# One pool of six PSUM banks for scores, first feed-forward products, masks and transposes, with score visits of one to three slots

## The chip, the core and the metric

The kernel runs on one core of a Trainium2 chip. The metric is the device time in microseconds from the start to the end of one execution; the figure for a kernel is the median of several runs. The profile is one profiled execution, with times in us from its first instruction. PE is the tensor engine, PEld its weight loads, DVE the vector engine, ACT the scalar engine, POOL is GpSimd, and SP issues most of the transfers. Each engine works through its own instructions in the order in which they were written into the program.

## The reference

Attention with a block mask, then a feed-forward layer with a squared relu:

```python
# q, k, v: 4 batches x 8 heads x 768 positions x 64
scores = scale * q @ k.T
scores = where(mask, scores, -1e9)        # blocks of 32: neighbours, edges, 3 sampled blocks per row
attn   = softmax(scores)
x      = (attn @ v), heads side by side   # 3072 tokens x 512
out    = relu(x @ w_in) ** 2 @ w_out      # 512 -> 2048 -> 512
```

## The kernel before

**Attention.** The 32 pairs of batch and head are handled two heads at a time, so there are 16 units `u`, four to a batch. A *slot* is one unit, one range of queries and two or three chunks of 128 keys. In batch 0 the first 256 queries come in two ranges of 128 with three chunks of keys (16 slots of 2 x 384 scores); everywhere else a slot is 256 queries by two chunks of keys (132 slots of 2 x 512 scores). A slot's scores are keys by queries and fill two PSUM banks, one per head. `scores` (L381) writes them: each matmul contracts over 64 rows, and the two heads sit in the upper and lower half of the array. `exps` (L399) is one exponential on ACT for both banks, into an SBUF tile `pT`. `masks` (L405) multiplies `pT` with the mask on DVE; the first 16 slots instead add the mask inside the scores with extra matmuls (L395). `values` (L420) multiplies `pT` with the values and a column of ones, 65 columns per matmul, into a bank `po` that is held for one range of queries. `normalize` (L435) divides by the sum on DVE, and the result is transposed to `xT`: in batch 0 by PE (`x_transp`, L444), later by a transposing transfer.

**Feed-forward.** Tokens come in tiles `T`: for batch 0 two of 128 and two of 256, for each later batch two of 384. `hidden` (L478) multiplies one chunk of 128 of the 2048 columns of `w_in` with `xT`, four matmuls deep, into a bank `ph`. At tiles of 128 tokens two chunks share a bank (`per_unit`, L475). `relu` (L488), on ACT or DVE, moves the bank to an SBUF tile `r` in float32; `square` (L497), on POOL or ACT, makes the bfloat16 tile `g`. `output` (L521) sums `g` times `w_out` over the 16 chunks into a bank `py`, in eight parts; `out_copy` and `store` take it out.

**PSUM.** There are eight banks. Before, four belong to the pool `ps` (two score tiles of two banks each, also used for `mask_rows`, L302), two to `ph` (first products, and the transposes `pt` and mask tiles `pk` of the opening), one to `po` and one to `py`.

**What sets the order.** Nothing is ordered by hand. Every step is a `Task` with an engine or a choice of engines with estimated durations, a key (its priority), the tasks it depends on, and the buffers it takes (`get`) and gives back (`put`). `run_schedule` (L119) simulates the engines and picks again and again the task that could start first, ties broken by key; tasks with a key under 100 (attention) go ahead of the rest within a margin `AHEAD`. A small hash (`tie`, `SEEDS`) shifts the keys. When a task is picked, its function is called and its instructions are written into the program. So the constants, the number of buffers and the seeds determine each engine's order, and the chip then runs that order with its real durations.

`attend` (L606) makes the tasks of a *visit*: the scores of one or two slots written together, since PE changes between contraction over 64 and over 128 rows around a visit. Before, batch 0 has visits of one slot for its first 128 queries and of two for the rest, and the later batches visits of two. `PACE0` and `PACE` give the earliest time at which a visit of batches 1 to 3 may start. `prepare` (L560) makes loads, casts and transposes of a unit; in batches 1 to 3 the transposes are transfers.

The feed-forward tasks are made at the end (L688 to L726): for each tile the first products of this tile and the output parts of the tile before are interleaved by key, and all may run beside attention as soon as their `xT` is there.

Of the kernel before, what the change touches and what calls it, by code (L numbers as in the profile page):

```python
# [19 lines left out]
P = 128  # L20
# [5 lines left out]
def kernel(  # L26
# [27 lines left out]
    TWM = 384  # L54
# [5 lines left out]
    PT_BUFS, R_BUFS, G_BUFS, XT_BUFS = 6, 4, 2 * NF + 2, 3  # L60
# [3 lines left out]
    ps_s = ctx.enter_context(tc.psum_pool(name="ps_s", bufs=2))  # L64
    ps_o = ctx.enter_context(tc.psum_pool(name="ps_o", bufs=1))
    ps_h = ctx.enter_context(tc.psum_pool(name="ps_h", bufs=2))
# [9 lines left out]
    CB, GATES = 0.4, (6, 7)  # L76
    QT0, ADDED, ALONE = [(0, 128), (128, 128), (256, 256), (512, 256)], (0, 128), (0, 128)
# [5 lines left out]
    AHEAD = {"PE": 0.021, "DVE": 0.089, "ACT": 0.144, "POOL": 0.0, "SP": 0.0}  # L83
    LEAD = 9.733
    PACE0, PACE, SINGLE, MASK_AT = 43.352, 1.684, 1, 17.0

    class Buf:
        def __init__(self, pool):
            self.pool, self.holds, self.free = pool, 0, 0.0
# [4 lines left out]
    TIES = 2.757, 2.707  # L94
    SEEDS = (
            997007, 734824, 532673, 925841, 745989, 714641, 109461, 798098, 925326,
            634149, 527289, 224329, 653624, 743444, 608088, 229557, 928387, 381331,
            84432, 104783, 194889, 255966, 621276, 580226, 46894, 921115)
# [6 lines left out]
    class Task:  # L105
        def __init__(self, engs, key, fn, deps=(), get=(), put=(), after=0.0, mode=None, dma=0.0, late=None, bias={}, port=False):
            self.engs = engs if isinstance(engs, dict) else dict([engs])
            self.key, self.fn = key, fn
            self.deps, self.get, self.put = list(deps), list(get), list(put)
            self.after, self.mode, self.dma, self.late, self.bias = after, mode, dma, late, bias  # L110
            self.port = port
            self.end = self.eng = None
            self.order = len(tasks)
            self.key += TIES[0 if key < 300 else 1] * tie(self.order)
            for b in self.put:
                b.holds += 1
            tasks.append(self)

    def run_schedule(free, bufs, dma_free, mode=128):  # L119
        taken = {name: [] for name in bufs}  # L120
        port = {"DVE": (0.0, 0.0), "POOL": (0.0, 0.0)}
# [7 lines left out]

        while waiting or ready:  # L130
            now = [t for t in waiting if all(d.end is not None for d in t.deps)]
# [5 lines left out]
            for t in ready:  # L137
                r0 = t.after
                ok = True
                cnt = {}  # L140
                for b in t.get:
                    held = taken[b.pool]
                    at = len(held) + cnt.get(b.pool, 0) - bufs[b.pool]
                    cnt[b.pool] = cnt.get(b.pool, 0) + 1
                    if at >= 0:
                        if held[at].holds:
                            ok = False
                            break
                        r0 = max(r0, held[at].free)
# [3 lines left out]
                for e, us in t.engs.items():  # L153
                    r = max([r0, free[e]] + [seen(d, e) for d in t.deps])
# [6 lines left out]
                found.append((round(opt[1], 4), t.key, t.order, t, opt))  # L161
                if t.key < 100:
# [3 lines left out]
                       key=lambda c: c[:3], default=None)  # L166
            assert best is not None, "no task can start"
# [19 lines left out]
            for b in t.get:  # L187
                taken[b.pool].append(b)
# [65 lines left out]
    junk = ps_h.tile([P, 512], F32, name="junk", tag="h")  # L254
    for _ in range(N_WARM):
        nc.tensor.matmul(junk[:, 0:256], warm[:, 0:P], warm, start=True, stop=True)
# [45 lines left out]
    def mask_rows(c0, c1, e):  # L302
        mtile["R"] = ps_s.tile([P, 1024], F32, name="pb", tag="ps")[:, 0:c1 - c0]
# [7 lines left out]
    def mask_tile(n, c0, c1, e):  # L311
        pk = ps_h.tile([P, 512], F32, name="pk", tag="h")[:, 0:c1 - c0]
# [26 lines left out]
    def transp(u, w, ns, e):  # L339
        src = cast.pop((u, w, ns.start))  # L340
        pt = ps_h.tile([P, NCH, P], BF, name="pt", tag="h")
# [39 lines left out]
    def scores(slots, add, e):  # L381
        for a in slots:
            u, q0, w, cs = a
            i = u % NPB
            ps = ps_s.tile([P, 2, 512], F32, name="ps", tag="ps")
# [88 lines left out]

    def per_unit(T):  # L475
        return 2 if T[2] == P else 1

    def hidden(T, f, half, e):  # L478
        b, c0, w = T
        n = per_unit(T)  # L480
        if half == 0:
            htile[T, f] = ps_h.tile([P, TWM], F32, name="ph", tag="h")[:, 0:w * n]
        work_ = [(f + i, i, kc) for i in range(n) for kc in range(KM)]
        for f_, i, kc in work_[half * len(work_) // 2:(half + 1) * len(work_) // 2]:
            nc.tensor.matmul(htile[T, f][:, i * w:(i + 1) * w], w_in_sb[:, kc, f_ * P:(f_ + 1) * P], xT[b][:, kc, c0:c0 + w],  # L485
                             start=(kc == 0), stop=(kc == KM - 1))

    def relu(T, f, e):  # L488
        r = work.tile([P, TWM], F32, name="r", tag="r", bufs=R_BUFS)[:, 0:T[2] * per_unit(T)]
        src = htile.pop((T, f))  # L490
        if e == "ACT":
            A.activation(out=r, in_=src, func=AF.Relu)  # L492
        else:
            V.tensor_scalar(out=r, in0=src, scalar1=0.0, scalar2=None, op0=AOP.max)  # L494
        rltile[T, f] = r

    def square(T, f, e):  # L497
        g = work.tile([P, TWM], BF, name="g", tag="g", bufs=G_BUFS)[:, 0:T[2] * per_unit(T)]
        r = rltile.pop((T, f))
# [4 lines left out]
        for i in range(per_unit(T)):  # L504
            gtile[T, f + i] = g[:, i * T[2]:(i + 1) * T[2]]
# [12 lines left out]
    def y_pool(T, i):  # L518
        return "h" if T == TILES[-1] and i % 2 else "y"

    def output(T, i, ts, cs, part, e):  # L521
        if part == 0:
            pool, tag = (ps_h, "h") if y_pool(T, i) == "h" else (ps_y, "y")
            ytile[T, i] = pool.tile([P, d_model], F32, name="py", tag=tag)[:, 0:cs[1] - cs[0]]
# [14 lines left out]
    def T_(engs, key, f, *args, **kw):  # L539
# [5 lines left out]
              (3, 0, 0): 9.8, (3, 1, 0): 10.9, (1, 2, 0): 11.9, (2, 2, 0): 13.0, (3, 2, 0): 14.0}  # L545
    arrive.update({(u, 0, 2): (15.1, 15.8, 16.4, 17.1)[u] for u in range(HP)})
# [13 lines left out]
    def prepare(u):  # L560
# [17 lines left out]
        else:  # L578
            at = dict(after=arrive[u, 2, 0])
            late_q = first_of_tile[u, 2 * P]  # L580
            for w, ns in [(1, ns) for ns in (KEYS if u == 0 else (ALL,))] + [(0, ns) for ns in QRS]:
# [4 lines left out]
                qc, hb = Buf("qc"), Buf("h")  # L586
# [6 lines left out]
                t = T_(("PE", 0.06 * n), key + 1, transp, u, w, ns, deps=[c], get=[hb], put=[qc], mode=128)  # L593
# [12 lines left out]
    def attend(group, add):  # L606
        s = min(order.index(a) for a in group)
        bufs = {a: Buf("ps") for a in group}
# [3 lines left out]
        sc = T_(("PE", (0.44 if add else 0.22) * area), s, scores, group, add,  # L612
                deps=deps + (mr[:1 + (group[-1][1] + group[-1][2] > QW)] if add else []) + sc_all[-1:], get=[bufs[a] for a in group], mode=64,
                after=PACE0 + PACE * (s - N0) * (1.06 - 0.0006 * (s - N0)) if s >= N0 else 0.0)
        sc_all.append(sc)
        for a in group:
# [5 lines left out]
            ex = T_(("ACT", 0.2 + 0.82 * part), s, exps, a, deps=[sc], get=[pt], put=[bufs[a]])  # L622
# [4 lines left out]
            va = T_(("PE", 0.245 * part), s + 3.009, values, a, deps=[ex] + cv[u] + va_all[-1:] + (kws if po_pool(u, q0) == "y" else []),  # L627
# [23 lines left out]
    for i, (c0, c1) in enumerate(((0, QW), (QW, S))):  # L651
        rb_ = Buf("ps")
        t = T_(("PE", 0.11 + 0.11 * i), 5.0 if i else -90.0, mask_rows, c0, c1, after=9.8 if i else 4.6, get=[rb_], put=[], mode=32)
# [6 lines left out]
    for us in [range(b * HP, (b + 1) * HP) for b in range(B)]:  # L660
# [3 lines left out]
        if us[0] < HP:  # L664
            for c0, c1, at in MASKED:
                for n in range(NCH):
                    mb, w = Buf("h"), (c1 - c0) / 512
                    t = T_(("PE", 0.216 * w), (2 * n + 30 if c0 == 0 else 2 * n + 2), mask_tile, n, c0, c1, get=[mb], mode=128, after=at, deps=mr)
# [3 lines left out]
            while mine:  # L672
                q0 = mine[0][1]
                n = 1 if q0 in ALONE or len(mine) == 1 else 2
                attend(mine[:n], q0 in ADDED)
                mine = mine[n:]
        else:
            for i in range(0, len(mine) - 1, 2):
                attend(mine[i:i + 2], False)
            if len(mine) % 2:  # L680
                attend(mine[-1:], False)

    HID = {256: 0.22, 384: 0.325}
    RELU = {256: {"DVE": 0.424, "ACT": 0.39}, 384: {"DVE": 0.557, "ACT": 0.49}}
    SQ = {256: {"POOL": 0.613, "ACT": 0.42}, 384: {"POOL": 0.826, "ACT": 0.52}}
    sq_of, n_key = {}, 1000.0
    gbuf, hbuf = {}, {}
    for k_, T in enumerate(TILES + [None]):  # L688
# [4 lines left out]
        for _, kind, x in sorted(both, key=lambda z: z[:2]):  # L693
# [3 lines left out]
            if kind == 0:  # L697
# [3 lines left out]
                hb, rb, gb = Buf("h"), Buf("r"), Buf("g")  # L701
                gbuf[x] = gb
                last_use = c0 + t[2] == S and f == NF - 1
                h0 = T_(("PE", HID[w]), n_key - 0.5, hidden, t, f, 0, deps=need + [wl[f * NWP // NF], wl[(f + per_unit(t) - 1) * NWP // NF]],
                        get=[hb], mode=128)
                h1 = T_(("PE", HID[w]), n_key - 0.6, hidden, t, f, 1, deps=[h0],
                        put=[xb[b]] if last_use else [], mode=128)
                rr = T_(RELU[w], 200, relu, t, f, deps=[h1], get=[rb], put=[hb], bias={"ACT": 0.276})
                sq = T_(SQ[w], n_key, square, t, f, deps=[rr], get=[gb], put=[rb], bias={"ACT": 0.533})
                sq_of.update({(t, f + i): sq for i in range(per_unit(t))})  # L710
            else:
# [7 lines left out]
                yy = T_(("PE", 0.432 * n), n_key, output, t, i, ts, cs, part,  # L719
# [3 lines left out]
                if part == NY - 1:  # L723
# [5 lines left out]
                 {"ps": 2, "po": 1, "h": 2, "y": 1, "pT": PT_BUFS, "r": R_BUFS, "g": G_BUFS, "ys": YS_BUFS,  # L729
# [31 lines left out]
```

## Time and profile before

Three runs took 273.89, 274.52 and 274.79 us; the median is 274.52. The profiled execution has a span of 273.3 us.

| group | count | busy us | mean ns |
|---|---|---|---|
| exponentials, 1024 wide, ACT (L402) | 132 | 127.8 | 1022 |
| exponentials, 768 wide over two banks, ACT (L402) | 16 | 12.4 | 812 |
| mask products, DVE (L409) | 132 | 102.3 | 789 |
| output products, 512 wide, PE (L526) | 368 | 97.2 | 379 |
| first products, 384 wide, PE (L485) | 384 | 78.7 | 326 |
| value products, PE (L431) | 1152 | 53.9 | 193 |
| scores, 256 wide, PE (L391) | 528 | 40.5 | 272 |
| relus 384 / 256 wide, ACT (L492) | 46 / 35 | 21.8 / 12.5 | 497 / 404 |
| relus 384 / 256 wide, DVE (L494) | 50 / 13 | 27.6 / 5.5 | 556 / 421 |
| squares 384 / 256 wide, POOL (L503) | 62 / 33 | 59.4 / 27.6 | 963 / 848 |
| squares 384 / 256 wide, ACT (L501) | 34 / 15 | 17.9 / 6.3 | 525 / 430 |

Busy time of a group is the union of its instructions, so it is less than the count times the mean where instructions overlap. Matmuls are pipelined and their recorded ends are modelled: the distance between the starts of two neighbours tells more than the length of one. An engine that is idle costs nothing unless the one that sets the pace waits for it.

### The profile page before, as it was taken

The page shows a single profiled execution, that of the slowest core. Times are in us where ns is not written, and L with a number is a line of the kernel's source. Part 1 is how long each engine was busy: PE and PEld are TensorE (multiplying, and loading weights), DVE is VectorE, ACT ScalarE, POOL GpSimd, SP SyncE. Part 2 cuts the span into 40 slices and gives each one's busy share as a digit, 9 for nine tenths or more (in the row PEclk, how much of TensorE's full clock was granted, in tenths as well). Part 3 has the DMA queues.
Part 4 walks back from the last instruction along what each step waited for, and adds up shares of the span by engine and source line. Part 5 has one row for each costly group of instructions (what it writes and reads, how often), then busy time and mean ns, then how long its engine had stood idle before and what let it go on. Part 6 is the DMA issues. An engine that isn't in the chain of part 4 may idle for free.

```text
span 273.3 us, 7473 instructions
## 1 busy us (share of the span) xinstructions
PE 265.3 (97%) x3032; PEld 163.4 (60%) x3032; DVE 190.2 (70%) x380; ACT 207.6 (76%) x321; POOL 109.9 (40%) x138
## 2 busy tenths in 40 slices
PE   8889999999999999999999999999999999999995
PEld 5658766676666555565556555555555555555544
DVE  7778779989786768889666877786666775434400
ACT  3788999999999879999998799889999881010111
POOL 3194651457545227444420270441411414666410
PEclk9999999999999999999999999999999999999999
DMA  6999999999990285499711132355210111111112
GB/s 180 374 226 196 201 264 288 304 300 339 192 232 14 83 156 159 79 251 245 218 56 51 55 77 50 79 108 60 67 52 19 50 20 50 38 40 41 38 70 83
DMA packets 51882, 36.92 MB, mean 135 GB/s; under 512 B 30984, under 2 KB 48904, under 8 KB 51848
## 3 DMA queue, kind: packets, MB, share of 16 engines
q1 hardware_dynamic: 47080, 31.86, 43.9%
q0 software_dynamic: 4224, 4.19, 9.7%
q8 instruction: 23, 0.38, 0.6%
q10 hardware_dynamic: 544, 0.39, 0.5%
q14 instruction: 11, 0.09, 0.1%
HBM read 27.26 MB, written 6.29 MB: 123 GB/s over the span
## 4 chain that ended last, share of the span: by engine, by line
PE 83%; DMA 9%; POOL 2%; SPq 2%; ACT 2%; issue 1%; ACTq 0%
PE py L526 30%; PE ph L485 29%; PE po L431 12%; PE ps L391 12%; DMA w_out_sb<-in_moe_w_out_dram 6%; DMA vs<-in_v_dram 3%; SPq L226 2%; POOL w_in_sb L365 1%; ACT pT L402 1%; POOL w_out_sb L368 1%; POOL VT L200 0%; ACT ys L198 0%; ACT xT L198 0%; PE pk L313 0%; PE po L448 0%
## 5 line engine op out<-in xcount | busy, mean ns | idle before, releaser
L402 ACT ACTIVATE pT<-ps 128x1024 bf16<-128x1024 f32 (+1 forms) x148 | 140.2, 1000 | 11.2 <-PE ps L391 7.5
L503 POOL TENSOR_TENSOR g<-r 128x384 bf16<-128x384 f32 (+1 forms) x95 | 87.0, 923 | 120.4 <-DVE r L494 61.7
L409 DVE TENSOR_TENSOR pT<-pT,MK 128x1024 bf16<-128x1024 bf16 x132 | 102.3, 789 | 16.4 <-ACT pT L402 15.9
L485 PE MATMUL ph<-xT,w_in_sb 128*128 128x384 bf16 (+2 forms) x640 | 106.4, 294 | 0.0
L526 PE MATMUL py<-w_out_sb,g 128*128 128x512 bf16 (+1 forms) x400 | 100.7, 371 | 0.3 <-DMA w_out_sb<-in_moe_w_out_dram 0.2
L485 PEld LDWEIGHTS <-w_in_sb 128*128 128x128 bf16 x640 | 52.1, 97 | 28.7 <-issue 5.0
L431 PEld LDWEIGHTS <-pT 128*128 128x128 bf16 x1152 | 47.4, 98 | 18.6 <-issue 5.3
L431 PE MATMUL po<-VT,pT 128*128 128x65 bf16 x1152 | 53.9, 193 | 1.5 <-POOL VT L200 1.2
L494 DVE TENSOR_SCALAR r<-ph 128x384 f32<-128x384 f32 (+1 forms) x63 | 33.1, 528 | 31.4 <-PE ph L485 28.8
L526 PEld LDWEIGHTS <-g 128*128 128x128 bf16 x400 | 36.2, 98 | 28.3 <-issue 2.9
L391 PE MATMUL ps<-QK 64*128 64x256 bf16 (+1 forms) x624 | 47.3, 263 | 0.5 <-ACT pT L402 0.5
L198 ACT COPY ys<-py 128x512 f32<-128x512 f32 (+1 forms) x23 | 13.1, 570 | 38.0 <-PE py L526 37.8
L391 PEld LDWEIGHTS <-QK 64*128 64x128 bf16 x624 | 24.9, 94 | 23.0 <-issue 19.4
L492 ACT ACTIVATE r<-ph 128x384 f32<-128x384 f32 (+1 forms) x81 | 34.3, 457 | 3.0 <-PE ph L485 2.8
L501 ACT ACTIVATE g<-r 128x384 bf16<-128x384 f32 (+1 forms) x49 | 24.1, 496 | 6.0 <-DVE r L494 4.8
L200 POOL CAST VT<-vs 128x768 bf16<-128x768 f32 x15 | 13.8, 918 | 26.4 <-PE po L431 14.5
L441 DVE TENSOR_TENSOR xq<-po,rs 128x256 bf16<-128x256 f32 (+1 forms) x52 | 21.0, 404 | 1.8
L439 DVE RECIPROCAL rs<-po 128x4 f32<-128x4 f32 (+1 forms) x52 | 9.2, 177 | 13.5 <-PE po L431 13.2
L200 DVE CAST qc<-qs 128x768 bf16<-128x768 f32 (+2 forms) x18 | 12.6, 703 | 0.2 <-DMA qs<-in_q_dram 0.2
L200 DVE CAST qc<-ks 128x768 bf16<-128x768 f32 (+1 forms) x15 | 9.0, 603 | 1.9 <-DMA ks<-in_k_dram 1.8
L395 PE MATMUL ps<-R,oh 64*128 64x128 bf16 x96 | 6.7, 216 | 0.0
L343 PE MATMUL pt<-identb,qc 128*128 128x128 bf16 x48 | 5.0, 228 | 1.1 <-DVE QK L200 0.8
(51 smaller groups left out, 62.9 us busy)
## 6 DMA issues: line engine op xcount, KB each, us to landing
vs<-in_v_dram SPq DMA_DIRECT2D x16, 384.0 KB, 6.4
out_dram<-ys SPq DMA_DIRECT2D x23, 256.0 KB, 2.1
ks<-in_k_dram SPq DMA_DIRECT2D x15, 384.0 KB, 5.0
qs<-in_q_dram SPq DMA_DIRECT2D x12, 384.0 KB, 4.1
w_in_sb<-in_moe_w_in_dram POOLq DMA_DIRECT2D x4, 512.0 KB, 7.9
w_out_sb<-in_moe_w_out_dram POOLq DMA_DIRECT2D x4, 512.0 KB, 16.0
qs<-in_q_dram SPq DMA_DIRECT2D x4, 256.0 KB, 8.4
xT<-xq SPq DMA_TRANSPOSE x36, 2.3
```

Source lines behind the costliest of these rows:

```text
L200: (V if e == "DVE" else G).tensor_copy(out=out, in_=in_)
L391: nc.tensor.matmul(ps[:, h, j * w:(j + 1) * w], QK[i][hs, 1, ksl], QK[i][hs, 0, qsl], start=j == 0, stop=not add, skip_group_check=True)
L402: A.activation(out=pT[:, :, 0:n], in_=stile.pop(a)[:, :, 0:n], func=AF.Exp, scale=scale)
L409: V.tensor_tensor(out=pT, in0=pT, in1=m[:, None].broadcast_to([P, 2, len(cs), w]), op=AOP.mult)
L431: nc.tensor.matmul(po[:, qc, h, :], pT[:, h, j * w + qc * P:j * w + (qc + 1) * P], VT[i][:, h, n, 0:VW], start=(n == 0 and qc == 0 and h = ...
L441: V.tensor_tensor(out=xq, in0=po[:, :, :, 0:D], in1=rs.broadcast_to([P, n, 2, D]), op=AOP.mult)
L485: nc.tensor.matmul(htile[T, f][:, i * w:(i + 1) * w], w_in_sb[:, kc, f_ * P:(f_ + 1) * P], xT[b][:, kc, c0:c0 + w], start=(kc == 0), stop= ...
L492: A.activation(out=r, in_=src, func=AF.Relu)
L494: V.tensor_scalar(out=r, in0=src, scalar1=0.0, scalar2=None, op0=AOP.max)
L501: A.activation(out=g, in_=r, func=AF.Square)
L503: (G if e == "POOL" else V).tensor_mul(out=g, in0=r, in1=r)
L526: nc.tensor.matmul(ytile[T, i], gtile[T, f][:, ts * P:(ts + 1) * P], w_out_sb[:, f, cs[0]:cs[1]], start=(f == 0), stop=(f == NF - 1))
```

## The change

The pools `ps` and `ph` become one set of three pairs of banks, `X[0]` to `X[2]`, six banks in all. A task asks for `X1` (one bank) or `X2` (a pair), and the scheduler's `bank` gives it the place that comes free first. Four things follow from it:

- Scores (`X2`) can have three slots in PSUM at once instead of two. `GROUPS` sets the number of slots in a visit by batch and range of queries: one in batch 0, two in batch 1, three in batches 2 and 3.
- First products of tiles of 384 tokens take a pair and cover two chunks, so that one relu handles 768 columns over two banks; smaller tiles fill one bank with 512 columns (`per_unit` 4 and 2). The squares stay 384 or 512 wide. The first products of a pair are written in four parts and may be interleaved with other work (`yields`, `HOLD`).
- Transposes, masks and every second output of the last tile take an `X1`.
- The scheduler's constants are others (`AHEAD`, `LEAD`, `PACE0`, `PACE`, `TIES`, `SEEDS`, the preference of relus and squares for their engines, the key of `values`), so the order of all engines changes.

What it is for: buffers that go where they are needed, fewer and larger relus, and fewer changes of the array between 64 and 128 rows in the later batches.

```diff
-    TWM = 384
+    TWM = 768
-    PT_BUFS, R_BUFS, G_BUFS, XT_BUFS = 6, 4, 2 * NF + 2, 3
+    PT_BUFS, R_BUFS, G_BUFS, XT_BUFS = 6, 4, 34, 3
-    ps_s = ctx.enter_context(tc.psum_pool(name="ps_s", bufs=2))
+    ps_x = ctx.enter_context(tc.psum_pool(name="ps_x", bufs=1))
-    ps_h = ctx.enter_context(tc.psum_pool(name="ps_h", bufs=2))
...
+    GROUPS = (1, 1, 1), (2, 2, 2), (3, 3, 3), (3, 3, 3)
-    AHEAD = {"PE": 0.021, "DVE": 0.089, "ACT": 0.144, "POOL": 0.0, "SP": 0.0}
-    LEAD = 9.733
-    PACE0, PACE, SINGLE, MASK_AT = 43.352, 1.684, 1, 17.0
+    AHEAD = {"PE": 0.043, "DVE": 0.108, "ACT": 0.176, "POOL": 0.0, "SP": 0.0}
+    LEAD = 5.943
+    HOLD = 0
+    PACE0, PACE, SINGLE, MASK_AT = 39.28, 1.726, 1, 17.0
...
+        def bank(pool, now, gone):
+            n = 2 if pool == "X2" else 1
+            best = None
+            for c in range(0, 6, n):
+                mine = [cells[i] for i in range(c, c + n)]
+                if any(i in gone for i in range(c, c + n)) or any(b and b.holds for b in mine):
+                    continue
+                r = max([now] + [b.free for b in mine if b])
+                o = cells[c ^ 1]
+                k_ = (round(r, 4), n == 1 and not (o and o.holds), c)
+                if best is None or k_ < best[0]:
+                    best = (k_, c, r)
+            return best
...
+                if t.yields and not relaxed and due - HOLD < opt[1]:
+                    continue
...
+    X = [ps_x.tile([P, 1024], F32, name=f"X{i}") for i in range(3)]
+
+    def bank_of(b):
+        return X[b.at // 2][:, b.at % 2 * 512:(b.at % 2 + 1) * 512]
...
-            ps = ps_s.tile([P, 2, 512], F32, name="ps", tag="ps")
+            ps = X[bufs[a].at // 2].rearrange("p (h c) -> p h c", h=2)
...
-            va = T_(("PE", 0.245 * part), s + 3.009, values, a, ...
+            va = T_(("PE", 0.245 * part), s + 2.023, values, a, ...
...
-                n = 1 if q0 in ALONE or len(mine) == 1 else 2
-                attend(mine[:n], q0 in ADDED)
...
+            n = min(len(mine), GROUPS[us[0] // HP][mine[0][1] // QW])
+            if n == 3:
+                n = sum(a[:2] == mine[0][:2] for a in mine)
+            attend(mine[:n], us[0] < HP and mine[0][1] in ADDED)
...
     def per_unit(T):
-        return 2 if T[2] == P else 1
+        return {P: 4, QW: 2, S // 2: 2}[T[2]]
...
-                h0 = T_(("PE", HID[w]), n_key - 0.5, hidden, t, f, 0, deps=..., get=[hb], mode=128)
-                h1 = T_(("PE", HID[w]), n_key - 0.6, hidden, t, f, 1, deps=[h0], ...)
-                rr = T_(RELU[w], 200, relu, t, f, deps=[h1], get=[rb], put=[hb], bias={"ACT": 0.276})
-                sq = T_(SQ[w], n_key, square, t, f, deps=[rr], get=[gb], put=[rb], bias={"ACT": 0.533})
+                wide = w > 512
+                hb, rb = Buf("X2" if wide else "X1"), Buf("r")
+                parts = 4 if wide else 2
+                for part in range(parts):
+                    hd.append(T_(("PE", HID[w] / parts), n_key - (0.6 if part else 0.5), hidden, t, f, part, parts, hb, ...,
+                                 mode=128, yields=not part))
+                rr = T_(RELU[w], 200, relu, t, f, deps=[h1], get=[rb], put=[hb], bias={"ACT": 0.092})
+                for i in range(0, per_unit(t), n):
+                    sq = T_(SQ[n * t[2]], n_key, square, t, f, i, n, deps=[rr], get=[gb], put=[rb], bias={"ACT": 0.673})
```

## The prediction

> **What bounds the kernel now.** I read the page's busy table first, then busy time by stage, then the waits, then single instructions in order of time. The page's own lines:
>
> ```profile
> PE 265.3 (97%) x3032; PEld 163.4 (60%) x3032; DVE 190.2 (70%) x380; ACT 207.6 (76%) x321; POOL 109.9 (40%) x138
> PE   8889999999999999999999999999999999999995
> ACT  3788999999999879999998799889999881010111
> ```
>
> The tensor engine (PE) is busy nearly everywhere, ScalarE (ACT) nearly everywhere until the last fifth. To see which sets the pace, I cut the span at the first scores of 256 queries (24 us), of batches 1, 2 and 3 (59, 112, 168) and after the last scores (223). The columns are the window, its length, and each engine's busy time:
>
> ```profile
> 5.00:24.00 19.00, 16.53 (x347) 12.87 (x348) 14.69 (x46) 14.70 (x25) 9.46 (x13) 1.00 1.06 275
> 24.00:59.00 35.00, 33.98 (x511) 24.50 (x507) 29.56 (x61) 33.55 (x60) 15.15 (x18) 1.00 1.12 272
> 59.00:112.00 53.00, 53.00 (x651) 33.74 (x649) 41.50 (x76) 48.73 (x78) 25.96 (x30) 1.00 0.71 164
> 112.00:168.00 56.00, 56.00 (x632) 32.62 (x628) 43.39 (x81) 51.70 (x77) 21.10 (x20) 1.00 0.48 126
> 168.00:223.00 55.00, 55.00 (x614) 31.44 (x608) 39.30 (x74) 48.88 (x69) 14.85 (x14) 1.00 0.28 58
> 223.00:273.00 50.00, 47.01 (x284) 25.70 (x280) 17.91 (x33) 8.21 (x14) 21.27 (x26) 1.00 0.15 51
> ```
>
> From 59 us on PE is never idle (53.00 of 53.00 and so on). Before 59 us ACT is nearly full as well (33.55 of 35.00 in the second row), and this is where PE loses time. The waits of PE alone, longest first:
>
> ```profile
> PE po L431 <- POOL VT L200: 1.2, 1, 1.2
> PE pt L343 <- DVE QK L200: 0.8, 2, 0.5
> PE ps L391 <- ACT pT L402: 0.5, 2, 0.3
> ```
>
> These are only part: matmul ends are modelled, so I counted starts. In order of time around a visit to the scores (start, length, engine, line):
>
> ```profile
> 132.25 1.14 PE L485 MATMUL ph<-xT,w_in_sb 128*128 128x384 bf16 x6
> 133.32 0.61 PE L391 MATMUL ps<-QK 64*128 64x256 bf16 x8
> 133.86 0.60 PE L526 MATMUL py<-w_out_sb,g 128*128 128x512 bf16 x2
> ```
>
> One 384-wide matmul takes 0.326 us, so six in 1.14 start (1.14 - 0.326) / 5 = 0.163 apart. 132.25 + 6 x 0.163 = 133.23, but the scores start at 133.32: 0.09 lost. Eight scores in 0.61 with 0.27 for the last pair are 4 pairs 0.11 apart, 0.44 in all, yet the next matmul comes after 0.54: 0.10 lost. So one visit to the scores costs 0.19 us beyond its matmuls.
>
> By the same reading of starts, one matmul costs 0.216 us at 512 columns, 0.162 at 384, 0.109 at 256, 0.055 at 128, 0.055 for a 256-wide score (two run at a time), 0.029 for a 128-wide one, and 0.0295 for a value product. Summed over all 3,032 that is 243.1 us; 78 visits x 0.19 add 14.8: **257.9 us of PE work**. PE runs from 1.2 to 270.0, 268.8 us, so it loses 10.9. Up to batch 1's first scores at 59.07 the work is 49.3: there it loses 59.07 - 1.2 - 49.3 = 8.6, of which some 1.4 is the slow pace of the 14 warm-up matmuls. After that 208.5 us of work take 210.9; the losses there are crumbs.
>
> **What the Trainium skill says.** "TensorEngine Tiling (Array Packing)", Key Properties: changing the tiling mode drains the array. The trace agrees: 0.09 into and 0.10 out of the 64-row scores. "Perfetto Trace Analysis", Identifying the Most-Contended Engine: matmul busy share is no measure of headroom. Agreed: PE reads 97%, but 10.9 us of its span are not work. The same page, Optimizing Scalar/DVE Operations: each ACT or DVE instruction carries a fixed access cost, so larger ones gain. Agreed: a relu on ACT takes 404 ns at 256 columns and 497 at 384, so 0.73 ns per column and some 218 fixed.
>
> **The change part by part.**
>
> *Visits.* I counted both instruction orders that the scheduler writes. The matmuls are the same 3,032 in kind and number. Visits go from 78 to 74: batches 2 and 3 need 12 each instead of 18, but batch 0 splits its pairs into singles. 4 x 0.19 = 0.76 us saved, on the path.
>
> *PE work before batch 1.* In the new order 52.3 us of PE work stand ahead of batch 1's first scores (49.3 before): a stretch of 162 matmuls, 12.2 us without a visit, stands at the end of batch 0. With three score buffers before the first 256-wide scores, and singles after it, the array gets first feed-forward products in while ACT works on exponentials. Against this, ACT must be no slower there. Its counts from the first 256-wide exponential to batch 1: before 24 exponentials, 18 relus of 256, 8 squares of 256, 4 masks, 5 copies to xT, 2 output copies; after 24, 12 of 512, 5 of 512, 3, 4, 1. Two exponentials take 1.92 us together at 1.02 each, so an instruction counts its length less 0.1. The row means 1.022, 0.404, 0.430, 0.384, 0.36, 0.589 give before 39.7 - 61 x 0.1 = 33.6 us, which is what the window shows (33.55). After, with relus of 512 at 0.59 (404 + 256 x 0.73) and squares of 512 at 0.62 (0.430 and 0.525 at 256 and 384, extended): 37.9 - 49 x 0.1 = 33.0. So ACT would reach batch 1 some 0.6 us sooner, at 58.5, if the opening were the same. PE: 1.2 start + 1.4 slow pace + 52.3 = 54.9; waits for loads and first operands that no order removes (1.2 for VT in part, 0.8, the 24-row mask matmuls and their mode) I take as 3.6, from the seven pauses that I find before 24 us: 58.5 too. Two engines that both must be on time rarely are; I put batch 1's first scores at 58.8. PE's loss before it is then 58.8 - 1.2 - 52.3 = 5.3 instead of 8.6: **3.3 us saved**.
>
> *Wide relus.* Half as many relus, at 768 over two banks: no row shows one on ACT. Below: 497 + 384 x 0.73 = 0.78 us; above: two of 384, 0.99. The 768-wide exponential over two banks takes 0.812; I take 0.80. Relus now nearly all run on ACT (65 of 72; 81 of 144 before), DVE drops from 63 to 7 and gets 17 output copies instead of 2. With lengths less 0.1, ACT does 42 us in batch 1 against 46.2 of PE work, 53 against 61.0 in batch 2, 48 against 55.0 in batch 3 (all up to the last scores): 87 to 92%, where it was 89 to 92%. Nothing on the path. In the tail ACT gets 13 relus and 13 squares, about 15 us of 42: hidden under PE.
>
> *Visits of three.* The new wait: three slots need all three bank pairs, so nothing of the first product can be written until an exponential has freed a pair, and the next visit needs the relu done. The cycle: the first slot's scores are readable 0.48 us after the visit starts (0.22 issue, rest drain), three exponentials 0.90 apart, relu 0.80, release 0.06: 0.48 + 2.7 + 0.8 + 0.06 = 4.04. The shortest cycle of PE in the new order has 3.49 + 0.66 + 0.19 = 4.34. With two relus and a square between, 4.04 + 0.7 + 0.41 = 5.15 against 5.7. First product behind slot 0: free at 0.48 + 1.02 + 0.06 = 1.56; PE has scores to 0.75 and usually four output matmuls to 1.61. Value and output products queue behind that wait, and ACT's relu behind them. So the slack is 0.05 to 0.3 us per visit. Bounds: 0, and 0.2 for each of 24 visits, 4.8. I take 0.5 in all.
>
> Sum: 0.76 + 3.3 - 0.5 = 3.6 us: 274.5 - 3.6 = **270.9 us**.
>
> **Rivals.**
> 1. *The early gain is not had.* ACT, at 33.55 of 35, holds PE back by the same 59 - 49.3 = 9.8, so moved-up work only pushes batch 1 later, to 62. Only the visits remain: 274.5 - 0.8 = 273.7. For it: ACT's own saving is 0.6 alone. Against: PE's pauses lie beside ACT work, and the new order puts matmuls there.
> 2. *Triples stall.* If each of 24 visits waits 0.2 us and the 17 single visits of batch 0 wait as much more, with the early gain halved: 274.5 - 0.8 - 1.6 + 4.8 + 3.4 = **280**; with 24 x 0.2 alone and no early gain 278.5. For it: slack 0.05 at the first product. Against: ACT's share falls in batches 1 and 2.
> 3. *The opening shrinks too*, since scores no longer wait for the second buffer: all pauses but load waits go, batch 1 starts at 57.5: 269.4.
>
> **How the numbers follow.** Forecast 0.56 (with its spread up to 272.5), rival 3 0.15, rival 1 0.14, rival 2 or milder stalls 0.15. The range runs from 268.8 (rival 3, with no stalls) to 274.2, rival 1 with a little stall; only rival 2 and the extreme of rival 3 lie outside. Faster 0.78 (forecast, rival 3 and the lucky half of rival 1), same 0.09, slower 0.13.
>
> **What would show it.** Right: batch 1's scores start at 58 to 59.5 with more first-product matmuls before them; 74 visits; PE without pauses from there on, 207 us to its end; ACT fuller in the tail. A 768-wide relu near 0.80. Wrong: PE waiting on ACT at the first product (`ph`) after visits of three, batch 1 starting past 61, or relus well over 0.9 us.

## The result, and the profile after

The changed kernel takes 277.41 us (median; 276.76 to 277.65), the kernel before 274.34 beside it: a ratio of 1.0108 [1.0083, 1.0134], slower by 3.1 us. The forecast was 270.9, faster by 3.6.

Most runs of one kernel lie within 1 us of its median; the 19 of the kernel before beside run 5 spread from 273.0 to 276.3. The profile of before has a long span for its kernel (273.3; the median of 19 runs is 272.3), that of after a short one (274.6; the median of four is 275.4). So the two profiles differ by 1.3 us where the kernels differ by 3.1.

The busy table and the slices of the kernel after:

```profile
PE 261.5 (95%) x2992; PEld 165.8 (60%) x3032; DVE 166.0 (60%) x339; ACT 224.2 (82%) x294; POOL 87.2 (32%) x110
PE   7989999889998999999999999999999999999995
ACT  3789999868997999999899989899798988646511
```

DVE has lost 24 us of work and ACT has gained 17, as the change of the relus intends. New are the slices with an 8 in PE's row at 48 to 62 and at 82 us, and with them a 6 in ACT's row at 55 us: both engines idle at the same time. (PE's count is 2,992 because records are missing from this trace, not matmuls from the program.) Busy time by stage, cut at the same events as before (first scores of 256 queries, of batches 1, 2 and 3, last scores):

```profile
5.00:22.70 17.70, 16.00 (x333) 12.54 (x331) 13.60 (x42) 14.11 (x25) 8.70 (x12) 1.00 1.06 279
22.70:62.80 40.10, 37.29 (x547) 26.52 (x549) 30.01 (x65) 35.30 (x50) 15.26 (x14) 1.00 1.15 275
62.80:111.20 48.40, 46.89 (x594) 30.28 (x602) 38.08 (x70) 44.10 (x54) 18.93 (x19) 1.00 0.52 145
111.20:173.00 61.80, 60.58 (x654) 36.91 (x666) 39.79 (x73) 57.10 (x72) 18.93 (x22) 1.00 0.48 122
173.00:228.00 55.00, 54.04 (x593) 33.10 (x604) 35.47 (x68) 49.18 (x61) 12.35 (x15) 1.00 0.26 60
228.00:274.60 46.60, 43.00 (x267) 23.96 (x266) 5.21 (x9) 22.58 (x34) 10.98 (x14) 0.99 0.14 49
```

Batch 1's first scores start at 62.8, not at 58.8 as forecast and not at 59.1 as before. In the second row neither PE (37.29 of 40.10) nor ACT (35.30) is full. The waits of PE, longest first, show a kind that the kernel before did not have: first products (L541) that wait for a relu on ACT (L550). And the waits of ACT show the reverse, relus that wait for first products:

```profile
PE X L541 <- ACT r L550: 2.5, 4, 0.8
PE py L585 <- issue: 1.9, 12, 0.2
PE X L308 <- DVE bm L298: 1.2, 1, 1.2
```

```profile
ACT r L550 <- PE X L541: 19.9, 32, 2.1
ACT ys L246 <- PE py L585: 5.3, 2, 4.2
```

To see where PE's time went, I priced its matmuls as in the prediction (0.216 us for 512 columns and so on, 0.19 per visit, missing records filled in) and took each stage's work from its length. What is left is PE's loss.

| stage, up to | before: work, loss | after: work, loss |
|---|---|---|
| first scores of 256 queries | 17.41, 5.72 | 16.57, 4.97 |
| batch 1 | 32.30, 2.45 | 35.69, 4.39 |
| batch 2 | 52.01, 0.65 | 46.27, 2.18 |
| batch 3 | 55.37, 0.68 | 61.03, 0.66 |
| last scores | 54.56, 0.59 | 54.89, 0.44 |
| end of PE | 46.70, 0.38 | 42.70, 0.38 |
| all | 258.35, 10.47 | 257.15, 13.02 |

In the profile after, forty records are missing, so the table is good to some 0.25 us. Counted instead from the order of the matmuls in the two programs, its first two rows are 17.23, 5.90 and 32.08, 2.67 before, and 16.38, 5.15 and 35.91, 4.18 after; the work before batch 1 is then the 49.3 and 52.3 of the prediction, and all work differs by 0.76, the four visits. By either count what is lost in addition is lost between 22.7 and 111 us, 3.0 to 3.5 us more there than before. The losses of the stages with visits of three are those of before. A second profile of the same kernel (the run *after_again* below) gives 5.47, 4.34 and 2.18 in the first three rows, so this is no draw of one execution.

### The profile page after: what moved, and what is told of

It reads as the page before. It is cut to its first block, busy times and chain, and to the rows that moved or that the text cites. A ratio compares the mean times of both kernels' runs of the same rounds, so it can differ in the third digit from the quotient of the medians.

```text
span 274.6 us, 7322 instructions
## 1 busy us (share of the span) xinstructions
PE 261.5 (95%) x2992; PEld 165.8 (60%) x3032; DVE 166.0 (60%) x339; ACT 224.2 (82%) x294; POOL 87.2 (32%) x110
## 4 chain that ended last, share of the span: by engine, by line
PE 86%; DVE 4%; ACT 4%; issue 2%; DMA 2%; SPq 1%; ACTq 0%; DVEq 0%
PE X L541 30%; PE py L585 27%; PE po L483 12%; PE X L443 12%; PE X L585 2%; DMA ks<-in_k_dram 2%; ACT r L550 1%; ACT pT L454 1%; DVE pT L461 1%; DVE QK L248 1%; SPq L274 1%; PE X L365 1%; PE po L500 1%; PE X L395 1%; PE X L447 0%
## 5 line engine op out<-in xcount | busy, mean ns | idle before, releaser
L454 ACT ACTIVATE pT<-X 128x1024 bf16<-128x1024 f32 (+1 forms) x148 | 137.8, 1006 | 7.9 <-PE X L443 5.3
L461 DVE TENSOR_TENSOR pT<-pT,MK 128x1024 bf16<-128x1024 bf16 x132 | 93.6, 729 | 24.3 <-ACT pT L454 23.5
L562 POOL TENSOR_TENSOR g<-r 128x384 bf16<-128x384 f32 (+1 forms) x65 | 59.2, 913 | 149.2 <-ACT r L550 128.1
L541 PE MATMUL X<-xT,w_in_sb 128*128 128x384 bf16 (+2 forms) x640 | 99.9, 294 | 2.9 <-ACT r L550 2.5
L585 PE MATMUL py<-w_out_sb,g 128*128 128x512 bf16 (+1 forms) x328 | 87.6, 374 | 3.4 <-issue 1.9
L541 PEld LDWEIGHTS <-w_in_sb 128*128 128x128 bf16 x640 | 54.3, 97 | 33.1 <-issue 6.7
L550 ACT ACTIVATE r<-X 128x768 f32<-128x768 f32 (+1 forms) x65 | 48.6, 754 | 22.4 <-PE X L541 19.9
L443 PE MATMUL X<-QK 64*128 64x256 bf16 (+1 forms) x624 | 46.6, 264 | 0.8 <-DVE MK L373 0.2
L248 DVE COPY ys<-py 128x512 f32<-128x512 f32 x17 | 11.6, 685 | 27.6 <-PE py L585 27.6
L246 ACT COPY ys<-py 128x512 f32<-128x512 f32 (+1 forms) x6 | 3.3, 558 | 5.5 <-PE py L585 5.3
L447 PE MATMUL X<-R,oh 64*128 64x128 bf16 x96 | 6.7, 216 | 0.0
```

The costliest lines, as they stand in the source:

```text
L248: (V if e == "DVE" else G).tensor_copy(out=out, in_=in_)
L443: nc.tensor.matmul(ps[:, h, j * w:(j + 1) * w], QK[i][hs, 1, ksl], QK[i][hs, 0, qsl], start=j == 0, stop=not add, skip_group_check=True)
L454: A.activation(out=pT[:, :, 0:n], in_=stile.pop(a)[:, :, 0:n], func=AF.Exp, scale=scale)
L461: V.tensor_tensor(out=pT, in0=pT, in1=m[:, None].broadcast_to([P, 2, len(cs), w]), op=AOP.mult)
L541: nc.tensor.matmul(htile[T, f][:, i], w_in_sb[:, kc, (f + i) * P:(f + i + 1) * P], xT[b][:, kc, c0:c0 + w], start=(kc == 0), stop=(kc == K ...
L550: A.activation(out=to, in_=src, func=AF.Relu)
```

## The experiments

**1. The bank that has been free longest.** The first suspect: the scheduler's `bank` gives out the place that comes free first, perhaps one whose relu has only just ended. The whole order is planned first, then written, with the oldest free place for each buffer. All engines keep their order.

```diff
-            t.fn(e)
+            plan.append((t, e))
+        write(plan)
...
+                        age = max([freed[id(m)] for m in mine if m], default=0)
+                        spots.append((age, c))
+                    b.at = min(spots)[1]
```

> The changed kernel with the order of every engine kept instruction by instruction; only the place in PSUM of each buffer differs: the bank or pair that has been free longest, instead of the lowest one that the scheduler reckons free at that moment. Theory 1 (first products wait because they are put into a bank whose relu the scheduler reckons done and the chip has not done): PE's waits for relus on ACT fall from 2.5 us to under 0.5, batch 1's first scores come at 60.5 instead of 62.8, the whole takes 274.8 to 275.8. Rival (ACT's throughput of relus and squares holds the stretch, whichever bank is used): batch 1 stays at 62.5 or later and the time within 0.5 us of the changed kernel's 277.4.

Measured: 276.90 us (276.62 to 277.45), ratio 1.0102 [1.0076, 1.0127]: at most 0.5 us of the 3.1, and the two intervals overlap. PE's waits for relus on ACT fall from 2.5 to 1.8 us and not below 0.5, and batch 1 starts at 63.5. So the age of the bank does not account for the loss. (This run moved pairs of banks as well, and its program has more of the waits found below, 55 against 50, so it does not weigh the age alone.)

**2. The wide relu cut in two.** If one relu of 768 columns over two banks holds both too long, two of 384 free the first earlier.

```diff
-            A.activation(out=to, in_=src, func=AF.Relu)
+        for i in range(n) if n * w > 512 else (slice(None),):
+            if e == "ACT":
+                A.activation(out=to[:, i], in_=src[:, i], func=AF.Relu)
```

> The changed kernel with each relu of 768 columns over two banks written as two relus of 384, on the same engine and in the same place; all else in the same order. If ACT's wide relus do no harm and save their fixed part (theory): 47 more instructions of 0.40 less 0.31 of a wide one's saved half, some 0.12 us each, so ACT gets 5 to 6 us more work in batches 2 and 3; with ACT at nine tenths there, PE begins to wait and the time rises by 2 to 5 us to 279.5 to 282. Rival (the two-bank relu itself is slow or holds banks too long and is where the time went): the time falls below 276.5, since the first bank comes free earlier.

Measured: 278.44 us (277.15 to 280.49), ratio 1.0161 [1.0115, 1.0207]. From batch 1's first scores to the end of PE it takes 208.55 us, as the changed kernel does (208.56). The first wide relu runs at 103 us, so what this run loses more stands ahead of all that was edited, and the intervals overlap. Neither forecast came true. The wide relus do not cause the loss, and they gain nothing either: the forecast gave ACT 5 to 6 us more work without them, but ACT is busy 224.0 us in this profile, with 47 more instructions, and 224.2 in that of the kernel after (the relus of 768 columns by themselves take 38.2 us, their halves 41.0).

**3. Other seeds for the changed kernel.** Is the order merely an unlucky one? The seeds were searched anew, to an order whose planned end is within 0.5 us.

```diff
-            621053, 621053, 621053, 162164, 486097, 621053, 621053, 88936, 279485,
...
+    SEEDS = (959464, 225077, 897217, 946755, 474903, 41602, 596199, 225377, ...
```

> The changed kernel with other seeds in the tie-breaking hash, searched until the scheduler reckons about the same end (0.5 us later), so another order of the same kind. If the loss comes from the mechanism (buffers reused the moment the scheduler reckons them free, batch 0's attention ahead of batch 1's operands): again slower than its reckoning, 276 to 279. If it was the luck of one order (rival): anywhere from 271 to 280, and as likely below the kernel before as above.

Measured: 278.39 us (278.08 to 278.51), ratio 1.0151 [1.012, 1.0181]. Batch 1's scores start at 65.5 us: another order, the same kind of loss in the same place.

**4. Other seeds for the kernel before.** Its seeds in reverse.

```diff
-            997007, 734824, 532673, 925841, 745989, 714641, 109461, 798098, 925326,
...
+    SEEDS = (921115, 46894, 580226, 621276, 255966, 194889, 104783, 84432, ...
```

> The kernel before with its seeds in reverse order and nothing else: an order nobody selected. The scheduler reckons it 5.0 us later than with its own seeds. If orders count for as much as the change (order-luck rival): 277 to 281, more than the whole difference to explain. If orders hardly count on the chip: within 1.5 us of 274.3.

Measured: 276.45 us (275.89 to 278.28), ratio 1.0074 [1.0049, 1.01], between the two forecasts. An unsearched order costs the kernel before 2 us; orders matter, but run 3 shows that one other searched order does not mend the changed kernel.

**What the single instructions say.** The timeline of the kernel after, in the stretch without visits before batch 1 (start, length, engine, line; in brackets the wait). Lines of other work are left out:

```profile
51.33 0.59 ACT L550 ACTIVATE r<-X 128x512 f32<-128x512 f32 x1
51.43 0.88 PE L541 MATMUL X<-xT,w_in_sb 128*128 128x128 bf16 x9
...
51.95 0.63 ACT L560 ACTIVATE g<-r 128x512 bf16<-128x512 f32 x1
...
52.48 0.58 ACT L550 ACTIVATE r<-X 128x512 f32<-128x512 f32 x1
...
53.09 0.63 ACT L560 ACTIVATE g<-r 128x512 bf16<-128x512 f32 x1
53.11 0.60 PE L541 MATMUL X<-xT,w_in_sb 128*128 128x256 bf16 x4 [0.81 <-ACT r L550]
```

The last line is the second half of a first product in bank 3 (`X[1]`, upper half). It waits until 53.06 for a relu that reads *bank 2*, the lower half of the same `X[1]`. Its own first half, among the nine matmuls from 51.43, did not wait: it had been written into the program before that relu, the second half after it. The compiled program says the same: each wait names a semaphore and a value, and the instruction that raises it can be looked up. In the changed kernel 50 waits (21 of PE, 15 of ACT, 14 of DVE) name an instruction that touches only the *other* bank of the same tile. (A wait that stands on an instruction of its own is counted with the instruction behind it.) In the kernel before there are none: there every one-bank buffer is a tile of its own. So the theory: the program's dependencies are kept per tile `X[i]`, not per bank, and two unrelated buffers in its halves run one after the other. The scheduler's own plan, which knows no such waits, ends PE at 266.1; replayed with them, at the planner's durations, the order ends PE at 271.7; measured is 271.4. The changed kernel even looks for such neighbours: of banks that are free by the same time, `bank` gives a one-bank buffer the one beside a bank in use (the second term of `k_`), so that pairs stay whole.

**5. Other pairs.** The order stays the same on every engine; each buffer's place comes from a list, searched so that the two halves of one tile are seldom in use together.

```diff
+    PLACES = ("0245240420142042014520142350124204201420420452402024052024020...
...
-            t.fn(e)
+            plan.append((t, e))
+        at = iter(PLACES)
+        for t, e in plan:
+            for b in t.get:
+                if b.pool in ("X1", "X2"):
+                    b.at = int(next(at))
+            t.fn(e)
```

> The instructions of the changed kernel in its order on every engine; only the bank that each one-bank buffer gets is another: chosen so that the two banks of one 1024-wide tile X[i] are seldom in use at once. In the changed kernel 50 waits are on an instruction that touches only the OTHER bank of the same tile (21 of TensorE, 15 of ScalarE, 14 of VectorE); here 26 are left, and none stands in the stretch between the end of batch 0's attention and batch 1's first scores. False sharing (the theory after three runs): the two banks of one tile are tracked as one thing, so a first product waits for the relu of its neighbour bank and that relu for the product: replaying the order with the planner's own durations gives an end of TensorE at 271.7 with such waits (measured 271.4) and 267.2 with this choice; batch 1's scores at about 60 instead of 62.8, a time of 272 to 273.5. Rival (ScalarE and TensorE in step because one unit of 512 costs both about the same, or late operands of batch 1): the choice of bank means nothing, batch 1's scores at 62.5 to 63.5, 276.5 to 277.5.

Measured: 274.06 us (273.31 to 275.41, 14 runs), ratio 0.9989 [0.9968, 1.0009]. The choice of places alone is worth 3.3 us, about all that the change had lost; the forecast for it (272 to 273.5, batch 1's scores at about 60) was too good: they start at 61.3. The same place in the timeline (its lines stand 9 further down):

```profile
51.53 0.60 ACT L559 ACTIVATE r<-X 128x512 f32<-128x512 f32 x1
51.79 1.65 PE L550 MATMUL X<-xT,w_in_sb 128*128 128x128 bf16 x19
...
52.16 0.63 ACT L569 ACTIVATE g<-r 128x512 bf16<-128x512 f32 x1
...
52.70 0.58 ACT L559 ACTIVATE r<-X 128x512 f32<-128x512 f32 x1
...
53.31 0.63 ACT L569 ACTIVATE g<-r 128x512 bf16<-128x512 f32 x1
...
53.39 1.04 PE L550 MATMUL X<-xT,w_in_sb 128*128 128x256 bf16 x8
```

Nineteen matmuls in a row, across the same relus and squares, without a wait. The waits of PE, longest first, no longer hold a first product behind a relu on ACT:

```profile
PE py L594 <- issue: 1.9, 12, 0.2
PE X L317 <- DVE bm L307: 1.2, 1, 1.2
PE X L452 <- DVE MK L382: 0.5, 1, 0.5
PE po L492 <- POOL VT L257: 0.4, 1, 0.4
PE X L550 <- DVE r L561: 0.3, 1, 0.3
```

And the stretch from the last scores of batch 0 to the first of batch 1, which holds the same matmuls, first in the kernel after, then with other pairs (window, length, busy PE, PEld, DVE, ACT, POOL):

```profile
47.70:62.80 15.10, 13.26 (x166) 10.39 (x166) 7.62 (x15) 11.08 (x19) 5.63 (x6) 1.00 1.16 301
```

```profile
48.38:61.28 12.90, 12.80 (x166) 10.40 (x166) 7.32 (x15) 10.68 (x19) 5.84 (x6) 1.00 1.16 303
```

PE is now full there: 12.80 of 12.90, so the stretch is 2.2 us shorter. Ahead of it, from the first scores of 256 queries, other pairs takes 25.62 us and the kernel after 24.98, and there ACT is as full as PE or fuller (kernel after first, then other pairs):

```profile
22.72:47.70 24.98, 24.01 (x381) 16.13 (x385) 22.39 (x51) 24.20 (x32) 9.63 (x9) 1.00 1.15 259
```

```profile
22.76:48.38 25.62, 24.19 (x382) 16.11 (x385) 22.95 (x51) 24.45 (x32) 8.95 (x9) 1.00 1.10 235
```

By the account of work and loss, other pairs loses 5.01, 2.83 and 1.19 us in the first three stages (after: 4.97, 4.39, 2.18) and 10.70 in all, about what the kernel before loses (10.47). The list moves buffers of two banks too: 53 of 196 lie in another pair than in the kernel after, 147 in run 7. So runs 5 and 7 weigh the places as a whole; run 6 changes the tiles and nothing else.

**6. The reverse, in the kernel before.** Its two one-bank buffers become the halves of one tile; banks, turns and order stay.

```diff
-    ps_h = ctx.enter_context(tc.psum_pool(name="ps_h", bufs=2))
+    ps_h = ctx.enter_context(tc.psum_pool(name="ps_h", bufs=1))
+    H = ps_h.tile([P, 1024], F32, name="H")
...
+    def next_h():
+        turn[0] ^= 1
+        return H[:, turn[0] * 512:(turn[0] + 1) * 512]
...
-            htile[T, f] = ps_h.tile([P, TWM], F32, name="ph", tag="h")[:, 0:w * n]
+            htile[T, f] = next_h()[:, 0:w * n]
```

> The kernel before in its own order, where the two one-bank buffers of the first products, masks and transposes are no longer two tiles but the two halves of one 1024-wide tile: same banks, same turns, same instructions. False sharing: 201 waits on the other half appear, almost all on first products and relus, and each makes a relu and the next product go one after the other, so it is slower by at least 3 us (277.5 or more; 290 if most of the 126 first-product units lose 0.15 us). Rival: waits follow banks and not tiles, 274.0 to 274.8 as before.

Measured: 302.44 us (301.9 to 303.59), ratio 1.1005 [1.0952, 1.1059]: 28 us for nothing but the way in which two banks are declared, and far more than the 290 that the forecast named as an upper case. The waits of PE:

```profile
PE H L492 <- DVE r L501: 12.7, 29, 0.7
PE H L492 <- ACT r L499: 4.3, 10, 0.9
PE H L350 <- DVE QK L200: 2.0, 3, 1.0
```

**7. The same pair.** The changed kernel's order once more; now a one-bank buffer goes beside a bank that is in use, if there is one.

```diff
-    PLACES = ("0245240420142042014520142350124204201420420452402024052024020...
+    PLACES = ("01234024023240241023454510432142042014240240120424214024214241242...
```

> The changed kernel's instructions in its order on every engine; now a one-bank buffer goes beside a bank that is in use where there is one (of several places the one free longest), so that neighbours share a tile as often as the order allows. False sharing: the opposite of the choice with other pairs, so slower than the changed kernel; replaying the order with the planner's durations ends TensorE at 274.9 (changed kernel 271.7, other pairs 267.2), so some 3 us more than 277.4: 279 to 282. Rival (the age of a bank or some other property of the single bank decides): the banks are no younger here than in the first experiment, 276.5 to 277.8.

Measured: 280.26 us (280.0 to 281.29), ratio 1.0216 [1.0186, 1.0246], inside the 279 to 282 of the theory and outside the rival. First products wait longer for relus than in the kernel after (2.5):

```profile
PE X L550 <- ACT r L559: 3.4, 5, 0.7
```

More of it is lost in the opening: the first scores of 256 queries come at 25.1 us, in the two profiles of the kernel after at 22.7 and 23.2. The program has hardly more shared waits (54 against 50), so it matters where they stand. So one order of instructions takes 274.1, 277.4 or 280.3 us by the places of its buffers.

**8. The changed kernel again,** beside 7 and 9, with nothing edited.

> The changed kernel once more, beside the others on one chip: 276.8 to 277.8, for a second profile of it. If its stretch without visits before batch 1 takes 14.5 to 15.5 us again, and 13.4 to 13.8 with other pairs, the difference is no draw of one profile.

Measured: 277.51 us (277.13 to 279.27), ratio 1.0128 [1.0088, 1.0167]. Its losses are told with the table above. The stretch before batch 1 takes 15.4 us (47.88 to 63.26), as forecast; with other pairs it is the 12.9 above. (The 13.4 to 13.8 of the forecast start at 47.7, which is 0.7 us ahead of those scores in run 5.)

**9. Order and places searched together.** A version to beat both: places in other pairs, and seeds, margins, pace and the preferences of engines searched again with the shared waits in the plan.

```diff
-    AHEAD = {"PE": 0.043, "DVE": 0.108, "ACT": 0.176, "POOL": 0.0, "SP": 0.0}
+    AHEAD = {"PE": 0.0381, "DVE": 0.0730, "ACT": 0.2408, "POOL": 0.0, "SP": 0.0}
...
-    TIES = 2.583, 1.777
+    TIES = 2.743, 1.462
+    SEEDS = (621053, 621053, 621053, 5165, 370792, 84889, 486721, 580236, ...
```

> A try at a version that beats both: places in other pairs as before, and order (seeds, margins, preferences of engines) searched again with the shared waits in the plan. The replay ends TensorE at 266.8, against 267.2 for other pairs alone, so 273.0 to 274.2; 273.7 taken. If the remaining loss lies in what the plan does not hold (arrivals in the opening), it stays at 274.1 or varies to 275.

Measured: 273.32 us (272.95 to 274.4, 13 runs), ratio 0.9965 [0.9947, 0.9984]: the one version that is faster than the kernel before, by 1 us.

## Why the prediction was wrong

*Visits: right.* 74 instead of 78 for 0.76 us. PE's work fell by 1.2 us in the table, where 40 records had to be filled in, and by just 0.76 in the count from the programs.

*PE work before batch 1: the step that failed.* The prediction had "PE's loss before it is then 58.8 - 1.2 - 52.3 = 5.3 instead of 8.6: 3.3 us saved". Measured by the same count, 62.81 - 1.2 - 52.3 = 9.3: a loss of 0.7 where a gain of 3.3 stood, 4.0 of the 4.9 us by which the two profiles miss the forecast (-0.76 + 0.7 + 1.36 = 1.3 slower where 3.6 faster was forecast; that the medians differ by 3.1 and not by 1.3 is the scatter told above). The prediction took six banks for six independent buffers. They are three tiles of two, and neighbours in a tile wait for each other: a second half of a first product for the relu of the bank beside it, and that relu for the first half. Run 6 shows it, and runs 5 and 7 show what it is worth here. In the stretch ACT's load was not at fault, for it has time over there (11.08 of 15.10). Nor was the opening: its loss of 4.97 is the 1.4 + 3.6 that the prediction gave it. What it left for the stage with the exponentials of 256 queries was 0.3; before lost 2.45 there, after 4.39, other pairs 2.83. So shared tiles account for about 1.6 of that stage, and the rest, as large as before, did not go away when the third score buffer came.

*ACT before batch 1: each length right, the sum too small.* Relus of 512 and squares of 512 are 0.60 and 0.63 in place of 0.59 and 0.62. But from the first scores of 256 queries to batch 1 ACT is busy 35.3 us (35.1 with other pairs) where the prediction had 33.0, and 57.1 in batch 2 where it had 53: the tenth that was taken off for each instruction was too much. The prediction also summed each engine over the whole way. By parts, ACT is nearly full up to the last scores of batch 0 (24.20 of 24.98 us, where PE has 23.3 us of work), and PE in the stretch, where its work is 12.6. An estimate from these figures is 22.7 + 24.2 + 12.6 = 59.5 for batch 1's first scores without any shared wait, later than the 58.8 of the prediction. No run tests this.

*After batch 1.* Forecast loss 0.5 more than before, for visits of three; measured 1.36 more (3.66 against 2.30), but in batch 1's stage, where the last one-bank first products of batch 0 still run (2.18 against 0.65; 1.19 with other pairs). The visits of three cost nothing: 0.66 and 0.44 in the stages of batches 2 and 3, against 0.68 and 0.59. There, first products, scores and exponentials all use whole pairs, and a tile has no stranger in its other half.

*Wide relus: right in size, and without effect on the time.* The rows by shape on ACT:

```profile
L454 ACT ACTIVATE pT<-X 128x1024 bf16<-128x1024 f32 x132 | 126.0, 1029 | 6.0 <-PE X L443 5.3 <-PE po L483 0.2
L550 ACT ACTIVATE r<-X 128x768 f32<-128x768 f32 x47 | 38.2, 812 | 16.9 <-PE X L541 14.5 <-POOL g L562 1.2
L550 ACT ACTIVATE r<-X 128x512 f32<-128x512 f32 x18 | 10.4, 600 | 5.5 <-PE X L541 5.4
```

0.81 us for 768 columns where 0.80 was taken. Run 2 shows that ACT's busy time is no shorter for it.

*The rivals.* Rival 1 (early gain not had, 273.7) is nearest in place. Its reason, a full ACT, is not what held PE in the stretch, and its sum misses that the change makes this stage worse. But with other pairs the time is 274.1, and ahead of the stretch ACT is nearly full: there the reason is not excluded. Rival 3, by its own terms, comes to 269.6 (270.9 less 1.3) and not to 269.4. Rival 2 had the right side for the wrong wait: visits of three did not stall. The range ended at 274.2. Of the signs that the prediction named against itself, one came true: batch 1 past 61, with PE waiting for ACT at first products, though after no visit at all.

*What stays open.* The miss is 6.7 us, and other pairs give back 3.3 of it: with 26 shared waits left in place of 50, and none in the stretch, the change is level with before (0.9989 [0.9968, 1.0009]), not 3.6 us faster. In the replay those 26, most on masks and transposes of batch 0, cost another 1.1 us (267.2 against 266.1). A version without any was not tried: an exponential reads both banks of a slot in one access, so a score buffer has to be one tile, and the other two banks are taken by `po` and `py`. That these waits, a full ACT ahead of the stretch and the old losses of batch 0 make up the rest is argued, not shown.

## What to carry to other kernels

When buffers of one and of two banks are to share a pool, look at what the program's dependencies are kept on. A tile that is handed out in halves couples the halves, and no simulated plan that thinks in banks will show it; the compiled program's waits do, before any run. If the halves must live in one tile, give concurrent users different tiles, and let the scheduler know of the coupling. And a larger instruction need not save time: ACT was busy as long in all with 94 relus of 384 columns as with 47 of 768.

## What was not expected of the hardware

Nothing in the engines: the lengths of single instructions came out as worked out, and only the overlap between ACT's instructions was smaller than taken. The 28 us of run 6 and the 3 us of the change are waits written into the program, not a conflict of the banks themselves: with other pairs, PE runs nineteen matmuls in 1.65 us beside relus that read other banks.
